# Output products woven between the half products of w_in, in a fused attention and feed-forward kernel

## The chip, the cores and the metric

The kernel runs on one core of a Trainium2 chip. The metric is the device time of one execution in microseconds (us). The engines are called PE (TensorE; its weight loads are shown apart as PEld), DVE (VectorE), ACT (ScalarE), POOL (GpSimd) and SP (SyncE, whose queue issues most transfers).

## The reference

Banded attention (each query sees itself and the 63 keys before it) over 8 batches, 8 heads, 576 positions and 64 columns a head; its result, as 4608 tokens of 512 columns, goes through two matrix products with a leaky ReLU of a slope per column between them:

```python
scores = scale * np.matmul(q, k.transpose(0, 1, 3, 2))
mask = (rel >= 0) & (rel < 64)
attn = softmax(np.where(mask, scores, -1e9))
x = (attn @ v) as (4608, 512)
h = x @ w_in                       # 512 x 2048
g = np.maximum(h, 0.0) + alpha * np.minimum(h, 0.0)
out = (g @ w_out).astype(np.float32)   # 2048 x 512
```

## The kernel before

**Tiles.** The 4608 tokens are 36 tiles of 128; four tiles make a batch (`ts`), nine batches in all (`n`). The 2048 columns between the products are 16 slices of 128 (`f`). Every matrix that goes into a product is held as a high and a low part ("h" and "l", both of type F32R), and a product is made of three: high by high, high by low, low by high.

**The two halves of the program.** Batches 0 and 1 go through `cell`, one slice at a time (L908). Batches 2 to 8 go through `pair`, which makes two slices at once: 7 batches of 8 pairs are 56 pairs. A pair makes the product of x with two slices of w_in out of seven half products instead of eight, from sums and differences of quarters of w_in (kept in DRAM by `combine`, and loaded again for each pair by `load`: the streamed blocks l0 to l4) and of x. A half product (`product`, L1038) is six matmuls of 128x128 weights with 256 columns. In the order of their steps they are: s12 (the first two in one step, so 12 matmuls; it waits for the block l0), s7, s6, s4, s5, s3. The last one needs what v2 adds on DVE from the result of s5. Copies on ACT carry parts of results on: c1 copies the result of s12 and s6 needs it, c7 that of s7 for s4, c6 that of s6 for s5.

**Behind a pair.** For each of its two slices `behind` runs a chain: slopes on ACT (L810), most on DVE (L817), high on ACT (gh, L823), rest on POOL (gl, L827), and the output matmuls (`outs`, L844): per tile gh by wout_h, gh by wout_l, gl by wout_h, 512 columns each, added in the tile's bank over all 16 slices. For pairs these 12 matmuls are three steps of four: gh, gh, gl.

**Attention** of the coming tiles is put in blocks between two pairs: scores (L586), values (L707), scores. It stands behind the last product of one pair and in front of the first of the next.

**The order.** Each step carries, per engine, how long it holds the engine and how long its result takes (`hold, lat`), what it waits for (`after`), what it stands behind in order alone (`behind`), which buffers it takes and gives, and a wish for its time (`want`). `Plan.order` lets a simulated machine, `Plan.run`, pick at each turn the step with the earliest due time (`late`) of those that can start first. The steps are then emitted in the order of the start times so found. Nothing is reordered after that on an engine. A half product holds PE for 0.72 in this plan, an output step for 0.2267 per matmul. Eight PSUM banks are used: four for outputs, four for the half products, scores and values.

Of the kernel before, what the change touches and what calls it, by code (L numbers as in the profile page):

```python
# [3 lines left out]

# [21 lines left out]
WARM = 28.0  # L26
SWITCH = 0.11
SLACK = 1.04


DUE = (
# [77 lines left out]
class Step:  # L109
    def __init__(self, engines, emit, after, behind, take, give, want, moved, span, port):  # L110
        self.engines, self.emit, self.after = engines, emit, [a for a in after if a is not None]
        self.behind, self.take, self.give, self.want, self.moved = behind, take, give, want, moved
        self.span, self.port = span, port
        self.before, self.tiled, self.next = [], False, None
        self.start = self.end = None
        self.late = math.inf


class Plan:
# [47 lines left out]
    def run(self, late):  # L167

        free = {PE: 0.0, DVE: 0.0, ACT: 0.8, POOL: 3.6, SP: 0.8, (DVE, "port"): 3.6, (POOL, "port"): 0.0}
        lanes, flying, tiled = 0.0, [], False  # L170
        left, base, ready, end = {}, {}, [], 0.0

        def open_up(s):
            wants = {}
            for b in s.take:
                wants[b.kind] = wants.get(b.kind, 0) + 1
            base[s] = (max([s.begin] + [a.end + HOP for a in s.after] + [a.start + 0.01 for a in s.behind]), wants)
            ready.append(s)

        for s, x in zip(self.steps, late):  # L180
            s.late, left[s] = x, len(s.after) + len(s.behind)
            if not left[s]:
                open_up(s)
        while ready:
            best = None
            picks = {}
            for s in ready:
                t0, wants = base[s]
                for kind, n in wants.items():
                    have = sorted(self.stock[kind])  # L190
                    t0 = max(t0, have[n - 1][0] + HOP if len(have) >= n else math.inf)
                if s.moved and len(flying) >= FLIGHT:
                    t0 = max(t0, flying[0])
                if t0 == math.inf:
                    continue
                for e in s.engines:
                    t = max(t0, free[e])
                    if e == POOL or s.port and e == DVE:
                        t = max(t, free[e, "port"])
                    picks.setdefault(e, []).append((t, s, e))  # L200
            for e, some in picks.items():
                first = min(x[0] for x in some)
                x = min((x for x in some if x[0] <= first + LOOK), key=lambda x: (x[1].late, x[0]))
                cost = (x[0], x[0] + x[1].engines[e][1], x[1].late)
                if best is None or cost < best[0]:
                    best = cost, x
            if best is None:
                return math.inf
            (_, (t, s, e)) = best
            while s:  # L210
                hold, lat = (x * (1.0 if e == PE else SLACK) for x in s.engines[e])
                while flying and flying[0] <= t:
                    heapq.heappop(flying)
                if e == PE and s.tiled != tiled:
                    tiled, hold, lat = s.tiled, hold + SWITCH, lat + SWITCH
                s.start, s.engine = t, e
                free[e] = t + hold
                if e == POOL or s.port and e == DVE:
                    free[DVE if e == POOL else POOL, "port"] = t + hold
                s.end = t + lat  # L220
                if s.moved:
                    lanes = max(lanes, t + hold + 0.65)
                    s.end = lanes + max(s.moved, s.span) + 0.45
                    lanes += s.moved
                    heapq.heappush(flying, s.end)
                end = max(end, s.end)
                for b in s.take:
                    have = self.stock[b.kind]
                    have.sort()
                    fit = [x for x in have if x[0] + HOP <= t + 1e-9]  # L230
                    x = fit[0]
                    have.remove(x)
                    b.at = x[1]
                for b in s.give:
                    b.uses -= 1
                    b.end = max(b.end, s.end)
                    if not b.uses:
                        self.stock[b.heir or b.kind].append((b.end, b.at))
                ready.remove(s)
                for b in s.before:  # L240
                    left[b] -= 1
                    if not left[b]:
                        open_up(b)
                s, t = s.next, free[e]
        return end

    def filled(self, done):
# [37 lines left out]
def banded_attention_then_prelu_ffn(  # L285
# [11 lines left out]
    nc = tc.nc  # L297
    P = 128
# [7 lines left out]
    NF = DFF // P  # L306
# [496 lines left out]
    def behind(ts, f, d, done, hb, want_o, cols, coarse=True):  # L803
# [28 lines left out]
        if f == NF - 1:  # L832
            todos = [every] if coarse else [every[j:j + 3] for j in range(0, 3 * n, 3)]
        else:
            todos = [gh_ones + gl_ones] if coarse else [gh_ones[:4], gh_ones[4:], gl_ones]

        def outs(todo):
            gh, gl = d["gh"], d.get("gl")
            for i, k in todo:
                t = ts[i]  # L840
                if f == 0 and k == 0:
                    po[t] = bank(ob[t], [P, E], F32, f"o_{t}")
                gt, wt = ((gh, "wout_h"), (gh, "wout_l"), (gl, "wout_h"))[k]
                nc.tensor.matmul(po[t], gt[:, cols[i] * P:(cols[i] + 1) * P], weight(wt, f),  # L844
                                 start=(f == 0 and k == 0), stop=(f == NF - 1 and k == 2))

        hold = {2: (1.46, 0.37, 0.40, 0.31, 0.69), 4: (2.72, 0.57, 0.667, 0.53, 1.24)}[n]
        lat = {2: (1.55, 0.475, 0.485, 0.405, 0.74), 4: (2.87, 0.69, 0.75, 0.62, 1.28)}[n]
# [11 lines left out]
        for todo in todos:  # L860
# [3 lines left out]
            s5 = step({PE: (h, h + 0.1)}, lambda _, todo=todo: outs(todo),  # L864
                      [s3] + [s4] * lows + cv[2 * f + 1]["done"], take=[ob[t] for t in own],
                      give=[ghb] + [glb] * lows, want=want_o)
            for x in {id(last_o[t]): last_o[t] for t in ts if t in last_o}.values():
                put_behind(s5, x)
            for t in ts:
# [129 lines left out]
    def pair(ts, q, want):  # L999
# [34 lines left out]
        def product(out, w, x, start):  # L1034
            todo = [(w[i], x[j]) for i, j in ((0, 0), (0, 1), (1, 0))]
            for i, (a, b) in enumerate(todo):
                for c in range(2):
                    nc.tensor.matmul(out, a[:, c * P:(c + 1) * P], b[c], start=start and i == c == 0,  # L1038
                                     stop=i == 2 and c == 1, skip_group_check=True)

        def p12(_):
            dx["h"] = bank(bx, [P, NBLK * P], F32, f"h_{ts[0]}_{f}")
            d["b"], d["a"] = dx["h"][:, :2 * P], dx["h"][:, 2 * P:]
            product(d["a"], own(0, 0), tokens(0, left), True)
            product(d["b"], streamed(0), tokens(1, left), False)

        def p7(_):
            dy["h"] = bank(by, [P, NBLK * P], F32, f"h_{ts[0]}_{f + 1}")
            d["d"], d["c"] = dy["h"][:, :2 * P], dy["h"][:, 2 * P:]
            product(d["d"], streamed(3), tokens(0, right), True)  # L1050

        def p6(_):
            product(d["a"], streamed(1), turned(2), False)

        def p5(_):
            product(d["a"], streamed(4), turned(0), False)

        def p3(_):
            product(d["a"], streamed(2), tokens(1, right), False)

        def p4(_):
            product(d["d"], own(1, 1), turned(1), False)

        def add(out, a, b):
            nc.vector.tensor_tensor(out=out, in0=a, in1=b, op=ALU.add)  # L1065
# [11 lines left out]
        (l0, b0), (l3, b3), (l1, b1), (l4, b4), (l2, b2) = (load(e) for e in (0, 3, 1, 4, 2))  # L1077
        x0, x1, x2, x3 = (st[t]["x"] for t in ts)
        one = {PE: (0.72, 0.91)}
        s12 = step({PE: (1.44, 1.63)}, p12, [st_done[t] for t in ts] + [l0], take=[bx], give=[b0, x0, x2], want=want)  # L1080
        s7 = step(one, p7, [l3], [s12], take=[by], give=[b3, x1, x3], want=want + 1.0)
        c1 = step({ACT: (0.28, 0.39)}, lambda _: spare(0, "a"), [s12], take=[u2])
        c7 = step({ACT: (0.28, 0.39)}, lambda _: spare(2, "d"), [s7], [c1], take=[u7])
        s6 = step(one, p6, [c1, l1], [s7], give=[b1, tsets[n]], want=want + 2.0)
        c6 = step({ACT: (0.28, 0.39)}, lambda _: spare(1, "a"), [s6, c1])
        s4 = step(one, p4, [c7], [s6], give=[tsets[n]], want=want + 3.0)
        s5 = step(one, p5, [c6, l4], [s4], give=[b4, tsets[n]], want=want + 4.0)
        v2 = step({DVE: (0.38, 0.48)}, lambda _: add(d["c"], d["a"], d["u7"]), [s5, c7, s4], give=[u7])
        s3 = step(one, p3, [v2, l2], give=[b2, x1, x3], want=want + 5.0)
        v3 = step({DVE: (0.38, 0.48)}, lambda _: add(d["d"], d["d"], d["u"][1]), [s4, c6, v2], give=[u2])  # L1090
        v1 = step({DVE: (0.38, 0.48)}, lambda _: add(d["b"], d["b"], d["u"][0]), [c1, s3], give=[u2])
        first[n, f] = first[n, f + 1] = s12
        last_p[n, f] = s3
        if q == 0:
            for b, m in zip((x0, x1, x2, x3), (1, 2, 1, 2)):
                b.uses = m * NF // 2
# [2 lines left out]
        behind(ts, f, dx, [s3, v1], bx, want + LAGS[0], cols, False)  # L1099
        behind(ts, f + 1, dy, [v2, v3], by, want + LAGS[1], cols, False)  # L1100

    tsets, loaded, last_p = {}, [], {}
    regions, taken, begun = {}, {}, []
    borrowed = [Buffer(f"x{i}", 4 * LENT) for i in range(NBLK)]
    for i, q0 in enumerate(TSETS):
# [58 lines left out]
    for n in range(NB):  # L1164
# [12 lines left out]
        for f in range(NF):  # L1177
# [11 lines left out]
            if (n, f) in stays:  # L1189
# [14 lines left out]
                    end = x  # L1204
                stay = f, end

    with tc.manual_schedule():
        for s in plan.order():
            s.emit(s.engine)


# [39 lines left out]
```

## Time and profile before

| what | value |
|---|---|
| three runs | 875.98, 877.21, 878.53 us, median 877.21 |
| the profiled execution | 877.72 us, of which a span of 876.0 us from the first to the last instruction |
| granted clock of TensorE | 1.000 of 2.4 GHz |
| busy share of the span | PE 99%, PEld 87%, DVE 64%, ACT 53%, POOL 41% |

A busy share tells how long an engine had at least one instruction under way. Matmuls overlap in the array, so that the spacing of their starts, not their durations, tells how fast they go.

### The profile page before, as it was taken

How to read it: one execution, taken by the hardware profiler on the slowest of the kernel's cores; microseconds unless marked ns; L12 is line 12 of the kernel's file. 1: busy time of each engine (PE TensorE's matmuls, PEld its weight loads, DVE VectorE, ACT ScalarE, POOL GpSimd, SP SyncE). 2: the span in 40 equal slices, each digit the busy share in tenths (PEclk: the TensorE clock that was granted, in tenths of full speed). 3: DMA queues.
4: the chain of work that ended last, by engine and by line, in shares of the span. 5: the costliest groups of instructions: out<-in, count | busy, mean ns of one | idle time of the engine just before them, and what ended most of it. 6: DMA issues, size and time to landing. Idle time of an engine off the chain costs nothing.

```text
span 876.0 us, 20755 instructions
## 1 busy us (share of the span) xinstructions
PE 867.1 (99%) x7793; PEld 764.2 (87%) x7793; DVE 557.2 (64%) x1611; ACT 465.4 (53%) x1245; POOL 359.0 (41%) x328
## 2 busy tenths in 40 slices
PE   8999999999999999999999999999999999999998
PEld 7888878888889898999898989989898989999997
DVE  5889978978675666657583848384856666423221
ACT  6888767456363636364544536363636363434333
POOL 4878665885433332333241333233323323222222
PEclk9999999999999999999999999999999999999999
DMA  9666857555765566645664576446655564345441
GB/s 312 196 191 198 255 148 240 152 176 172 246 202 167 149 190 195 191 136 164 211 190 131 151 237 202 141 131 216 196 166 148 190 196 130 110 126 175 121 121 61
DMA packets 106739, 153.93 MB, mean 176 GB/s; under 512 B 8704, under 2 KB 64272, under 8 KB 106640
## 3 DMA queue, kind: packets, MB, share of 16 engines
q1 hardware_dynamic: 105904, 151.95, 56.2%
q8 instruction: 62, 1.02, 0.5%
q10 hardware_dynamic: 736, 0.66, 0.2%
q14 instruction: 37, 0.30, 0.1%
HBM read 132.65 MB, written 19.92 MB: 174 GB/s over the span
## 4 chain that ended last, share of the span: by engine, by line
PE 97%; DVE 1%; DMA 1%; ACT 1%; issue 0%; POOL 0%; ACTq 0%; DVEq 0%; POOLq 0%
PE o L844 45%; PE h L1038 32%; PE h L908 10%; PE av L707 4%; PE s L586 3%; PE s L568 1%; DMA q<-qT 1%; PE t L664 1%; PE spare L377 0%; ACT w L616 0%; DVE w L610 0%; DVE two L412 0%; ACT pt L669 0%; POOL w L647 0%; ACTq L510 0%
## 5 line engine op out<-in xcount | busy, mean ns | idle before, releaser
L827 POOL TENSOR_TENSOR gl<-g,gh 128x512 fp32r<-128x512 f32 x128 | 165.5, 1294 | 409.4 <-ACT gh L823 244.3
L844 PE MATMUL o<-wout_h,gh 128*128 128x512 f32 x576 | 228.2, 396 | 0.0
L844 PE MATMUL o<-wout_l,gh 128*128 128x512 f32 x576 | 225.6, 392 | 0.0
L810 ACT ACTIVATE g<-h,sa_sb 128x512 f32<-128x512 f32 (+1 forms) x148 | 100.2, 677 | 160.9 <-DVE h L1065 139.0
L844 PE MATMUL o<-wout_h,gl 128*128 128x512 f32 x576 | 159.5, 390 | 0.0
L687 DVE STREAM_TRANSPOSE pt<-w 32x256 f32<-32x256 f32 x312 | 129.4, 427 | 6.0 <-POOL w L647 0.8
L844 PEld LDWEIGHTS o<-wout_h,gl 128*128 128x128 f32 x576 | 107.9, 188 | 23.2
L844 PEld LDWEIGHTS o<-wout_h,gh 128*128 128x128 f32 x576 | 108.5, 188 | 20.9 <-issue 0.5
L817 DVE SCALAR_TENSOR_TENSOR g<-h,s_sb,g 128x512 f32<-128x512 f32 x128 | 95.8, 749 | 45.2 <-ACT g L810 42.3
L844 PEld LDWEIGHTS o<-wout_l,gh 128*128 128x128 f32 x576 | 108.5, 188 | 18.4
L823 ACT CAST gh<-g 128x512 fp32r<-128x512 f32 x128 | 79.5, 621 | 79.4 <-DVE g L817 79.4
L1065 DVE TENSOR_TENSOR h<-h,w 128x256 f32<-128x256 f32 x56 | 24.2, 432 | 142.8 <-PE h L1038 142.4
L626 ACT ACTIVATE w<-w,nm 128x96 f32<-128x96 f32 x208 | 75.6, 366 | 15.5 <-DVE nm L620 15.5
L647 POOL TENSOR_TENSOR w<-w,rc 128x768 f32<-128x768 f32 (+2 forms) x44 | 59.3, 1348 | 56.5 <-DVE rc L643 53.8
L1075 ACT COPY u<-h 128x256 f32<-128x256 f32 x112 | 41.8, 373 | 76.2 <-PE h L1038 76.1
L1065 DVE TENSOR_TENSOR h<-h,u 128x256 f32<-128x256 f32 x112 | 48.0, 428 | 31.0 <-PE h L1038 25.6
L1038 PE MATMUL h<-xh,win_l 128*128 128x256 f32 x336 | 67.5, 283 | 0.0
L1038 PE MATMUL h<-xh,win_h 128*128 128x256 f32 x336 | 67.5, 282 | 0.0
L1038 PE MATMUL h<-win_h,win_l 128*128 128x256 f32 x336 | 58.8, 283 | 0.0
L1038 PEld LDWEIGHTS h<-xh,win_h 128*128 128x128 f32 x336 | 55.1, 191 | 3.4
L1038 PEld LDWEIGHTS h<-xh,win_l 128*128 128x128 f32 x336 | 53.1, 192 | 0.9
L1038 PE MATMUL h<-win_h,win_h 128*128 128x256 f32 x252 | 51.5, 295 | 0.1
(122 smaller groups left out, 1528.5 us busy)
## 6 DMA issues: line engine op xcount, KB each, us to landing
win_h<-kept SPq DMA_DIRECT2D x112, 256.0 KB, 3.0
win_l<-kept SPq DMA_DIRECT2D x112, 256.0 KB, 2.9
v<-vN SPq DMA_DIRECT2D x72, 256.0 KB, 4.6
stream<-kept SPq DMA_DIRECT2D x56, 256.0 KB, 2.7
k<-kT SPq DMA_DIRECT2D x35, 384.0 KB, 4.2
out<-os SPq DMA_DIRECT2D x35, 256.0 KB, 3.2
q<-qT SPq DMA_DIRECT2D x34, 256.0 KB, 4.3
raw<-w_in SPq DMA_DIRECT2D x16, 512.0 KB, 4.7
```

Source lines behind the costliest of these rows:

```text
L626: nc.scalar.activation(w, w, AF.Exp, scale=-1.0, bias=d["nm"][:, g:g + 1], accum_out=d["sm"][:, g:g + 1])
L647: nc.gpsimd.tensor_tensor(out=w, in0=w, in1=d["rc"][:, g].unsqueeze(2).broadcast_to(list(w.shape)), op=ALU.mult)
L687: nc.vector.transpose(dst[:, :, i * SUB:(i + 1) * SUB], d["w"][r, :, :, k * SUB:(k + 1) * SUB].rearrange("p e h k -> p (e h) k"))
L810: nc.scalar.activation(d["g"], d["h"][:, :nt], AF.Copy, scale=sa_sb[:, f:f + 1])
L817: nc.vector.scalar_tensor_tensor(out=g, in0=d["h"][:, :nt], scalar=s_sb[:, f:f + 1], in1=d["g"], op0=ALU.mult, op1=ALU.max)
L823: nc.scalar.copy(d["gh"], d["g"])
L827: (nc.vector if start else nc.gpsimd).tensor_tensor(out=d["gl"], in0=d["g"], in1=d["gh"].bitcast(F32), op=ALU.subtract)
L844: nc.tensor.matmul(po[t], gt[:, cols[i] * P:(cols[i] + 1) * P], weight(wt, f), start=(f == 0 and k == 0), stop=(f == NF - 1 and k == 2))
L908: nc.tensor.matmul(ph[:, :nt], weight(wt, f)[:, c * P:(c + 1) * P], tokens_of(xt, xs)[:, c], start=(k == 0), stop=(k == 3 * NP - 1))
L1038: nc.tensor.matmul(out, a[:, c * P:(c + 1) * P], b[c], start=start and i == c == 0, stop=i == 2 and c == 1, skip_group_check=True)
L1065: nc.vector.tensor_tensor(out=out, in0=a, in1=b, op=ALU.add)
L1075: nc.scalar.copy(d["u"][i], d[x])
```

## The change

Output steps of pairs become groups of three matmuls (`todos`). Half products (kind "h", now seven steps a pair, s12 split into s1 and s12) and output groups (kind "o") can be mated by the planner: when it picks one of them and one of the other kind could start at that time, both are emitted as one, an output matmul in front of every two of the half product. A half product takes a mate only when more than `keep` output groups have their inputs ready; `KEEP` gives that number for each of the seven. The plan counts a mated couple as `GAIN` = 0.024 shorter than its parts. The first half product doesn't wait for the streamed block any more, and stands behind the sixth product of the pair before (`before[-1:]`). The times of the three copies in the plan are lengthened.

```diff
+GAIN = 0.024
+KEEP = (1, 1, 1, 1, 1, 2, 2)
...
+        outs = [s for s in self.steps if s.kind == 'o']
...
+            if s.kind:
+                mates = [x for x, t0 in times.items() if x.kind and x.kind != s.kind and t0 <= t]
+                s.mate = min(mates, key=lambda x: x.late, default=None)
+                if s.mate:
+                    x = s if s.kind == "h" else s.mate
+                    fit = [o for o in outs if o.start is None and all(a.end is not None and a.end <= t for a in o.after)]
+                    if len(fit) <= x.keep:
+                        s.mate = None
+                if s.mate:
+                    s.next, s.mate.next, s.mate.mate = s.mate, s.next, s
...
+                if s.mate and not twin:
+                    twin = s.mate
+                    both = hold + s.mate.engines[e][0] - GAIN
+                    hold, lat = both, lat - hold + both
+                elif s is twin:
+                    hold, lat, twin = both, lat - hold + both, None
...
-            todos = [gh_ones + gl_ones] if coarse else [gh_ones[:4], gh_ones[4:], gl_ones]
+            todos = [gh_ones + gl_ones] if coarse else [(gh_ones + gl_ones)[j:j + 3] for j in range(0, 3 * n, 3)]
...
+            if not coarse:
+                s5.kind = "o"
...
-        s12 = step({PE: (1.44, 1.63)}, p12, [st_done[t] for t in ts] + [l0], take=[bx], give=[b0, x0, x2], want=want)
+        s1 = step(one, p1, [st_done[t] for t in ts], before[-1:], take=[bx], give=[x0], want=want)
+        s12 = step(one, p2, [l0], [s1], give=[b0, x2], want=want + 0.5)
...
-        c1 = step({ACT: (0.28, 0.39)}, lambda _: spare(0, "a"), [s12], take=[u2])
-        c7 = step({ACT: (0.28, 0.39)}, lambda _: spare(2, "d"), [s7], [c1], take=[u7])
+        c1 = step({ACT: (0.28, 0.46)}, lambda _: spare(0, "a"), [s12], take=[u2])
+        c7 = step({ACT: (0.28, 0.44)}, lambda _: spare(2, "d"), [s7], [c1], take=[u7])
...
-        c6 = step({ACT: (0.28, 0.39)}, lambda _: spare(1, "a"), [s6, c1])
+        c6 = step({ACT: (0.28, 0.44)}, lambda _: spare(1, "a"), [s6, c1])
...
-        first[n, f] = first[n, f + 1] = s12
+        first[n, f] = first[n, f + 1] = s1
+        for x, m in zip((s1, s12, s7, s6, s4, s5, s3), KEEP):
+            x.kind, x.keep = "h", m
...
+        before.append(s5)
...
+    def weave(some, others):
+        for _ in others:
+            for _ in range(2):
+                next(some)
+        for _ in some:
+            pass
...
         for s in plan.order():
-            s.emit(s.engine)
+            if s.mate and s.kind == "o":
+                continue
+            some = s.emit(s.engine)
+            if s.kind or inspect.isgenerator(some):
+                weave(some, s.mate.emit(PE) if s.mate else ())
```

`product` and `outs` yield after each matmul, so that `weave` can take an output matmul, then two of the half product, and so on.

## Rows read from the trace of the kernel before

**Rows 1.** The page: busy time per engine, and the chain that ended last.
```profile
PE 867.1 (99%) x7793; PEld 764.2 (87%) x7793; DVE 557.2 (64%) x1611; ACT 465.4 (53%) x1245; POOL 359.0 (41%) x328
...
PE 97%; DVE 1%; DMA 1%; ACT 1%; issue 0%; POOL 0%; ACTq 0%; DVEq 0%; POOLq 0%
PE o L844 45%; PE h L1038 32%; PE h L908 10%; PE av L707 4%; PE s L586 3%; PE s L568 1%; DMA q<-qT 1%; PE t L664 1%; PE spare L377 0%; ACT w L616 0%; DVE w L610 0%; DVE two L412 0%; ACT pt L669 0%; POOL w L647 0%; ACTq L510 0%
```
**Rows 2.** Windows: length, busy of PE, PEld, DVE, ACT, POOL, clock, DMA.
```profile
248.00:862.00 614.00, 613.20 (x5628) 552.50 (x5625) 356.36 (x1030) 293.11 (x791) 188.39 (x169) 1.00 0.55 165
```
**Rows 3.** Waits of PE from 225 us on: total, times, longest.
```profile
PE s L586 <- issue: 0.7, 3, 0.3
PE h L1038 <- DVE h L1065: 0.6, 1, 0.6
```
**Rows 4.** Chain in order of time, 480 to 530: start, length, what.
```profile
483.72 4.41 PE h L1038 x36
...
494.34 4.37 PE h L1038 x36
498.71 2.74 PE o L844 x12
501.44 0.71 PE h L1038 x6
502.16 2.75 PE o L844 x12
...
516.91 2.87 PE h L1038 x24
519.78 0.93 PE o L844 x4
...
521.42 2.73 PE o L844 x12
```
**Rows 5.** Timeline of PE, 493.9 to 505: start, length, matmuls that follow each other.
```profile
494.65 0.40 PE L1038 MATMUL h<-xh,win_l 128*128 128x256 f32 x2
...
496.09 0.40 PE L1038 MATMUL h<-xh,win_l 128*128 128x256 f32 x2
496.32 0.47 PE L1038 MATMUL h<-win_h,win_h 128*128 128x256 f32 x2
496.63 0.40 PE L1038 MATMUL h<-win_l,win_h 128*128 128x256 f32 x2
...
499.24 0.39 PE L844 MATMUL o<-wout_l,gh 128*128 128x512 f32 x1
...
501.28 0.40 PE L1038 MATMUL h<-xh,stream 128*128 128x256 f32 x2
501.51 0.40 PE L1038 MATMUL h<-xl,stream 128*128 128x256 f32 x2
501.75 0.40 PE L1038 MATMUL h<-xh,stream 128*128 128x256 f32 x2
```
**Rows 6.** Timeline of PE: the first matmuls of a run of four outputs.
```profile
519.62 0.39 PE L844 MATMUL o<-wout_h,gh 128*128 128x512 f32 x1
519.85 0.39 PE L844 MATMUL o<-wout_l,gh 128*128 128x512 f32 x1
```
**Rows 7.** Timeline of weight loads: the first two of s6, in the pair from 494.18.
```profile
496.29 0.30 PEld L1038 LDWEIGHTS h<-win_h,win_h 128*128 128x128 f32 x2
```
**Rows 8.** Timeline of ACT: the copy c1 of that pair.
```profile
495.86 0.37 ACT L1075 COPY u<-h 128x256 f32<-128x256 f32 x1 [1.45 <-PE h L1038]
```
**Rows 9.** Timeline of DVE: v2 of that pair.
```profile
498.81 0.43 DVE L1065 TENSOR_TENSOR h<-h,w 128x256 f32<-128x256 f32 x1 [0.92 <-PE h L1038]
```
**Rows 10.** Chain in order of time: the last run of matmuls.
```profile
862.27 10.07 PE o L844 x44
```
**Rows 11.** Timeline of ACT: the last cast to gh.
```profile
864.40 0.62 ACT L823 CAST gh<-g 128x512 fp32r<-128x512 f32 x1 [0.35 <-DVE g L817]
```
**Rows 12.** Timeline of weight loads: the first output behind a run of h.
```profile
501.88 0.19 PEld L844 LDWEIGHTS o<-wout_h,gh 128*128 128x128 f32 x1
```

More of the change, by code (lines that the diff above doesn't have):

```diff
@@ L1 @@
 import heapq
+import inspect
 import math
@@ L113, in __init__ @@
         self.span, self.port = span, port
-        self.before, self.tiled, self.next = [], False, None
+        self.before, self.tiled, self.next, self.kind, self.mate, self.keep = [], False, None, None, None, 0
         self.start = self.end = None
@@ L183, in run @@
                 open_up(s)
+        outs = [s for s in self.steps if s.kind == 'o']
         while ready:
             best = None
-            picks = {}
+            picks, times = {}, {}
             for s in ready:
@@ L195, in run @@
                     continue
+                times[s] = t0
                 for e in s.engines:
@@ L209, in run @@
             (_, (t, s, e)) = best
+            if s.kind:
[8 more added lines that the diff above has]
+                    s.next, s.mate.next, s.mate.mate = s.mate, s.next, s
+            twin = None
             while s:
@@ L243, in run @@
                         open_up(b)
-                s, t = s.next, free[e]
+                s, t = s.next, t if twin else free[e]
         return end
@@ L843, in outs @@
                 gt, wt = ((gh, "wout_h"), (gh, "wout_l"), (gl, "wout_h"))[k]
-                nc.tensor.matmul(po[t], gt[:, cols[i] * P:(cols[i] + 1) * P], weight(wt, f),
-                                 start=(f == 0 and k == 0), stop=(f == NF - 1 and k == 2))
+                yield nc.tensor.matmul(po[t], gt[:, cols[i] * P:(cols[i] + 1) * P], weight(wt, f),
+                                       start=(f == 0 and k == 0), stop=(f == NF - 1 and k == 2))
         hold = {2: (1.46, 0.37, 0.40, 0.31, 0.69), 4: (2.72, 0.57, 0.667, 0.53, 1.24)}[n]
@@ L1037, in product, with p1, p2 @@
                 for c in range(2):
-                    nc.tensor.matmul(out, a[:, c * P:(c + 1) * P], b[c], start=start and i == c == 0,
-                                     stop=i == 2 and c == 1, skip_group_check=True)
-        def p12(_):
+                    yield nc.tensor.matmul(out, a[:, c * P:(c + 1) * P], b[c], start=start and i == c == 0,
+                                           stop=i == 2 and c == 1, skip_group_check=True)
+        def p1(_):
             dx["h"] = bank(bx, [P, NBLK * P], F32, f"h_{ts[0]}_{f}")
             d["b"], d["a"] = dx["h"][:, :2 * P], dx["h"][:, 2 * P:]
-            product(d["a"], own(0, 0), tokens(0, left), True)
-            product(d["b"], streamed(0), tokens(1, left), False)
+            yield from product(d["a"], own(0, 0), tokens(0, left), True)
+        def p2(_):
+            yield from product(d["b"], streamed(0), tokens(1, left), False)
         def p7(_):
@@ L1049, in p7 @@
             d["d"], d["c"] = dy["h"][:, :2 * P], dy["h"][:, 2 * P:]
-            product(d["d"], streamed(3), tokens(0, right), True)
+            yield from product(d["d"], streamed(3), tokens(0, right), True)
         def p6(_):
-            product(d["a"], streamed(1), turned(2), False)
+            yield from product(d["a"], streamed(1), turned(2), False)
         def p5(_):
-            product(d["a"], streamed(4), turned(0), False)
+            yield from product(d["a"], streamed(4), turned(0), False)
         def p3(_):
-            product(d["a"], streamed(2), tokens(1, right), False)
+            yield from product(d["a"], streamed(2), tokens(1, right), False)
         def p4(_):
-            product(d["d"], own(1, 1), turned(1), False)
+            yield from product(d["d"], own(1, 1), turned(1), False)
         def add(out, a, b):
@@ L1100, in pair @@
         behind(ts, f + 1, dy, [v2, v3], by, want + LAGS[1], cols, False)
-    tsets, loaded, last_p = {}, [], {}
+    tsets, loaded, last_p, before = {}, [], {}, []
     regions, taken, begun = {}, {}, []
```

## The prediction

> **What bounds the kernel now.** I read the page first: TensorE is busy 99% of the span, and the chain that ended last lies on it for 97%, most of that in the output matmuls of L844 and the half-product matmuls of L1038 [rows 1]. The stage in which the change works runs from about 232 us to the end; for its main part the windows view gives TensorE 613.20 of 614.00 us busy, at a granted clock of 1.00 (2.4 GHz) throughout [rows 2]. The view of waits leaves TensorE with little more than 1 us of idle time there [rows 3]. So nothing is to be had from another engine; the time is a sum of matmul spacings, and the only question is whether the same matmuls in another order stand closer together. A busy share can't answer that, because a matmul that starts late behind its weight load, or waits inside the array, still counts as busy. So I went on to the chain in order of time, which gives the runs of equal matmuls and their lengths [rows 4], and to the starts in the timeline [rows 5, 6].
>
> A usual pair of 42 half matmuls (h) and 24 output matmuls (o) takes 4.37 us for 36 h, 2.74 for 12 o, 0.71 for the last six h, 2.75 for 12 o: 10.57 us [rows 4]. In the middle of a run, twelve h take 496.09 - 494.65 = 1.44 us, 0.120 each; nine o (499.24 to 501.28) take 2.04, 0.2267 each [rows 5]. At these spacings a pair would take 42 x 0.120 + 24 x 0.2267 = 10.48. The 0.09 above that is of two kinds:
>
> - A stall in the run of 36 h. The load that opens the fourth product, s6, stands at 496.29 [rows 7], where the last matmul of the product before starts at 496.21 (the row of two from 496.09) and a load elsewhere follows that start at once. It waits for the copy c1, which ends at 495.86 + 0.37 = 496.23 [rows 8]. Two h then take 496.63 - 496.32 = 0.31 instead of 0.24 [rows 5]. That is 0.07 a pair, in 43 of the 56 pairs; 11 of these have 4.41 instead of 4.37. The other 13 have the run cut, as 18 and 24 h, and the 24 take 2.87, less than 24 x 0.120 = 2.88 [rows 4].
> - The borders. The first two h behind an o take 0.23 (501.28 to 501.51), the next two 0.24 [rows 5], and six take 0.71 instead of 0.72 [rows 4]: an h run gives back about 0.008. Against this the 12 o behind it take 2.74 or 2.75 instead of 2.72, and four take 0.93 instead of 0.907 [rows 4]. An o run pays 0.015 to 0.03, some 0.003 to 0.007 for each of its first matmuls.
>
> **The change part by part.** No matmul, copy or transfer is added or left out. The matmuls of a pair stand as o, h, h, o, h, h in place of long runs.
>
> *How much is woven.* A pair has seven half products and eight output groups of three. A product is woven only when more groups are ready than its KEEP asks for. Behind the sixth product, v2 must run before the seventh: the run of h ends at 494.34 + 4.37 = 498.71 [rows 4], v2 at 499.24 [rows 9], and the load of the next product comes behind that. One group of 3 x 0.2267 = 0.68 us hardly covers the 0.53; KEEP leaves two. That leaves six groups for weaving, which I take: 18 trios of o, h, h, one product alone, two groups alone. Over 56 pairs that is 1008 trios; the first pair has no such groups in front of it, which I let pass.
>
> *What a trio costs.* The trace before has no single o between h, so I bound it. In long runs a trio is 0.2267 + 0.240 = 0.467. Lower end: both h stand first behind an o and give back 0.008, and the o, with only two h before it, pays nothing: 0.459. Upper end: the o pays the most that one matmul of a short run shows beyond that, and the h give nothing back: 0.475. The nearest row is the shortest o run, four o between h: its first takes 519.85 - 519.62 = 0.23 [rows 6], so 0.003 are paid; the h give back 0.008 as all 45 runs of six do. I take 0.462.
>
> *Sum.* A woven pair: 18 x 0.462 = 8.32, one product alone 0.71, two groups alone 1.36 + 0.02 = 1.38; together 10.41. The stall isn't in it: c1 has a woven s7 of 1.38 us behind it instead of 0.72, and the later copies likewise; where a product goes unwoven for want of groups, the 0.07 comes back. Against 10.57 that is 0.16; in the 13 cut pairs 0.09; 11 pairs had 0.04 more to lose. 43 x 0.16 + 13 x 0.09 + 11 x 0.04 = 8.5 us.
>
> *What is given back at the end.* Now 44 o stand behind the last h for 10.07 us [rows 10], and the last gh is made from 864.40 to 865.02 [rows 11], 2.8 us into that run, so that it is covered. With the older groups woven away, two groups (1.36) and those of the other cell stand there; that cell's cast ends 1 us before the last one's. I count 0.6 us of idle time. Some pairs will find fewer groups; 0.4 for that. Net gain 7.5 us.
>
> *Parts at no cost.* Splitting the first two products apart frees the first from its wait for the streamed block, and puts it behind the sixth product of the pair before. No wait for that block shows above the waits named [rows 3], so I count nothing; its price, were transfers late, is a wait in the second product instead. The regrouped outputs ask for gl one group sooner; POOL is busy 41% [rows 1], and first groups of other cells cover it. Both h banks of a pair are held longer; that is the rival below.
>
> The profiled execution took 877.72 us with a span of 876.0; the median of the three runs is 877.21. Gains are differences, so I take them from the median: 877.2 - 7.5 = 869.7, said as **869.5**. The three runs spread over 0.3%, so 0.3% (2.6 us) is about what a measurement tells from no change.
>
> **Rivals.**
>
> *The trio gives its full 0.459.* Then 1008 x 0.003 = 3.0 us more: 866.5. For it: an o at the end of a run shows no payment. Against: every first o behind h shows some.
>
> *The weave returns nothing.* A weight load starts as the matmul before it starts: the load for the o behind two h stands at 501.88, the second of the two h from 501.75 at 501.87 [rows 5, 12]. So only one load is ever ahead, and what an h can hide is the load behind it. In six h and three o, six loads stand behind an h and three behind an o, woven or not. If the load sets the 0.120, a trio stays at 0.467: 5.0 us less gained, 874.5, from the stalls alone. Against: the 0.23 above.
> The Trainium skill, TensorE: Matmul & The Clock Gate, section LDWEIGHTS, puts a load at its columns over 1.2 GHz, an estimate of 107 ns for 128, as long as 256 columns take at 2.4 GHz. By that rule the weave has nothing to hide better and the time is 874.5; the trace agrees in so far as h stand at 0.120 and not lower.
>
> *Slower: the attention blocks lose their cover.* Twelve blocks stand between two pairs, behind the last product of one and in front of the first of the next. In front of one stand 12 o, 2.73 us [rows 4], while DVE and ACT bring the finished pair out of its two banks, which the scores and values need. Woven, perhaps two groups (1.36) stand there. If nothing else is ready, 2.73 - 1.36 = 1.4 us are idle in each: 12 x 1.4 = 16 us, 886. It decides from 7.5 / 12 = 0.6 us a block. Against: a pair's first cell is finished before its last product and brings groups of its own. A trio at 0.475 would end there too: 1008 x 0.013 = 13 us, 882.5.
>
> **How the numbers follow.** Chances: 0.44 for the forecast, 0.24 for the full 0.459, 0.18 for no return, 0.14 for slower. The forecast's case reaches from 867 to 872. The range takes in 866.5 with 4 us below it (more groups woven, or a trio of 0.455), and 874.5 with 3 above: 862.5 to 877.5. No return falls about evenly on both sides of 0.3%: faster 0.44 + 0.24 + 0.07 = 0.75, same 0.11, slower 0.14.
>
> **What would show it.** In the timeline of the changed kernel: starts of o to o, over two h, of 0.46 (right), 0.467 (no return), over 0.47 (wrong sign); the load at the fourth product no longer late; a pair near 10.4 us; waits of TensorE below 3 us in all, at the end above all. If idle time stands around L586 and L707, the blocks are the cause; if pairs show half of their products alone, too few groups were ready and my 1008 is wrong.

## The result and the profile after

The changed kernel takes 881.69 us (four runs, 881.40 to 882.02) against 876.60 for the kernel before measured beside it; the ratio is 1.0051, with a 95% interval from 1.0037 to 1.0065. It is 0.5% slower, clear of that interval, where 869.5 was forecast, and it lies outside the range.

The profiled execution took 881.4 us, with a span of 879.7. The page (busy time, and the waits that the page puts in front of a group of L866, the old L844; L1062 is the old L1038, L904 the copy of a finished output tile to `os`):

```profile
PE 867.7 (99%) x7793; PEld 759.5 (86%) x7793; DVE 557.9 (63%) x1605; ACT 463.3 (53%) x1251; POOL 359.9 (41%) x328
...
PE 84%; DMA 5%; DVE 2%; ACT 2%; issue 1%; POOL 0%; ACTq 0%; DVEq 0%; POOLq 0%
...
L866 PE MATMUL o<-wout_h,gh 128*128 128x512 f32 x576 | 228.8, 397 | 4.0 <-ACT os L904 3.9
```

TensorE has the same busy share as in [rows 1], but the chain that ended last now leaves it: 5% go to a DMA, which was 1% (by the page's next line 3% of the span is stores, out<-os, and the rest transfers near the start), and an output matmul waits for ACT. The 3% aren't the loss: TensorE works on beside most of a store. In the view of waits of the whole changed kernel (total, times, longest) and, under it, of the kernel before:

```profile
ACT os L904 <- DMA out<-os: 16.1, 8, 2.3
PEld o L866 <- ACT os L904: 5.2, 6, 1.0
PE o L866 <- ACT os L904: 3.9, 5, 0.8
```

```profile
DVE os L882 <- DMA out<-os: 4.8, 3, 1.7
...
ACT os L880 <- DMA out<-os: 0.2, 1, 0.2
```

One of these places in the changed kernel, first in the chain in order of time, then in the timelines of SP, ACT and TensorE:

```profile
329.87 4.41 DMA out<-os
...
334.38 0.59 ACT os L904
...
335.02 3.02 PE o L866 x12
```

```profile
328.47 0.34 SPq L909 DMA_DIRECT2D out<-os  x1
...
329.87 3.01 SPq L909 DMA_DIRECT2D out<-os  x2
```

```profile
331.93 0.59 ACT L904 COPY os<-o 128x512 f32<-128x512 f32 x1 [2.17 <-PE o L866]
334.38 0.59 ACT L904 COPY os<-o 128x512 f32<-128x512 f32 x1 [1.86 <-DMA out<-os]
```

```profile
331.52 0.40 PE L866 MATMUL o<-wout_h,gl 128*128 128x512 f32 x1
331.75 0.40 PE L1062 MATMUL h<-win_h,win_l 128*128 128x256 f32 x2
331.99 0.39 PE L866 MATMUL o<-wout_h,gh 128*128 128x512 f32 x1
...
333.38 0.39 PE L1062 MATMUL h<-xh,win_h 128*128 128x256 f32 x2
333.61 0.40 PE L1062 MATMUL h<-xl,win_h 128*128 128x256 f32 x2
333.84 0.40 PE L1062 MATMUL h<-xh,win_h 128*128 128x256 f32 x2
335.02 0.50 PE L866 MATMUL o<-wout_h,gh 128*128 128x512 f32 x1 [0.78 <-ACT os L904]
```

This is the change from one batch to the next. The four output tiles of the old batch are copied to `os`, which has two buffers, and stored. The store issued at 329.87 lands 4.41 us later; only then can the fourth copy begin (334.38), which frees the fourth output bank. The old batch's last output matmul starts at 331.52, and the new batch's first one, at 331.99, stands only two h behind it. The first two output groups of the new batch (six o) find the three banks that are free; then comes a half product that isn't woven (six h); and the third group, which opens a run of 12 o, needs the fourth bank and stands on TensorE with everything behind it. Without the wait it would have started 0.12 behind the last h, at 334.08: 0.94 us are lost. There are five such places, some 94 us apart, and a smaller one; the weight loads are idle for 5.2 us there.

The same place in the kernel before, in the timelines of DVE and TensorE:

```profile
331.50 1.34 DVE L882 COPY os<-o 128x512 f32<-128x512 f32 x2 [1.61 <-DMA out<-os]
```

```profile
330.13 0.39 PE L844 MATMUL o<-wout_h,gl 128*128 128x512 f32 x1
...
333.23 0.39 PE L844 MATMUL o<-wout_h,gh 128*128 128x512 f32 x1
...
335.33 0.40 PE L844 MATMUL o<-wout_h,gh 128*128 128x512 f32 x1
```

A copy waits for a store here too. But 24 h stand between the old batch's last output matmul (330.13) and the new batch's first (333.23), and the last copy ends at 332.84, 2.5 us before the fourth bank is asked for (335.33).

The woven part itself, in the timeline of TensorE and of the weight loads in the changed kernel:

```profile
326.85 0.40 PE L866 MATMUL o<-wout_l,gh 128*128 128x512 f32 x1
...
328.25 0.39 PE L866 MATMUL o<-wout_l,gh 128*128 128x512 f32 x1
328.48 0.40 PE L1062 MATMUL h<-win_l,win_h 128*128 128x256 f32 x2
328.72 0.40 PE L866 MATMUL o<-wout_h,gl 128*128 128x512 f32 x1
...
331.52 0.40 PE L866 MATMUL o<-wout_h,gl 128*128 128x512 f32 x1
```

```profile
328.26 0.42 PEld L1062 LDWEIGHTS h<-win_l,win_h 128*128 128x128 f32 x2
328.60 0.19 PEld L866 LDWEIGHTS o<-wout_h,gl 128*128 128x128 f32 x1
328.72 0.42 PEld L1062 LDWEIGHTS h<-win_h,win_h 128*128 128x128 f32 x2
```

Ten trios, from 326.85 to 331.52, take 4.67 us, 0.467 each; the mean over the 800 trios between others is 0.468. That is the long runs' 0.2267 + 0.240 [rows 5], not 0.462. The o takes 0.23, the two h 0.24. As before ([rows 12]) each load stands at the start of the matmul in front of it.

Pair by pair: the first half product of the first pair starts at 226.21 (before 227.35), and from there to the end of the span it is 653.5 us against 648.7, 4.8 more. The waits for a bank give some 5.0 of that.

### The profile page after: what moved, and what is told of

It is laid out like the page before. It is cut to its first block, busy times and chain, and to the rows that moved or that the text cites. A ratio compares the mean times of both kernels' runs of the same rounds, so it can differ in the third digit from the quotient of the medians.

```text
span 879.7 us, 20764 instructions
## 1 busy us (share of the span) xinstructions
PE 867.7 (99%) x7793; PEld 759.5 (86%) x7793; DVE 557.9 (63%) x1605; ACT 463.3 (53%) x1251; POOL 359.9 (41%) x328
## 4 chain that ended last, share of the span: by engine, by line
PE 84%; DMA 5%; DVE 2%; ACT 2%; issue 1%; POOL 0%; ACTq 0%; DVEq 0%; POOLq 0%
PE o L866 41%; PE h L1062 29%; PE h L932 7%; PE av L729 4%; DMA out<-os 3%; PE s L608 3%; DMA raw<-w_in 1%; DMA raw<-w_out 1%; ACT os L904 1%; PE s L590 0%; DVE os L906 0%; DVE g L839 0%; DVE h L1091 0%; ACT two L432 0%; ACT u L1101 0%
## 5 line engine op out<-in xcount | busy, mean ns | idle before, releaser
L866 PE MATMUL o<-wout_h,gh 128*128 128x512 f32 x576 | 228.8, 397 | 4.0 <-ACT os L904 3.9
L866 PE MATMUL o<-wout_l,gh 128*128 128x512 f32 x576 | 226.6, 393 | 0.0
L866 PE MATMUL o<-wout_h,gl 128*128 128x512 f32 x576 | 194.7, 393 | 0.0
L866 PEld LDWEIGHTS o<-wout_h,gh 128*128 128x128 f32 x576 | 108.2, 188 | 17.2 <-ACT os L904 5.2
L866 PEld LDWEIGHTS o<-wout_h,gl 128*128 128x128 f32 x576 | 107.0, 188 | 11.8
L866 PEld LDWEIGHTS o<-wout_l,gh 128*128 128x128 f32 x576 | 108.6, 188 | 9.5
L1062 PE MATMUL h<-xh,win_h 128*128 128x256 f32 x340 | 67.6, 280 | 0.0
L1062 PEld LDWEIGHTS h<-xh,win_h 128*128 128x128 f32 x340 | 61.1, 188 | 6.7
L1062 PE MATMUL h<-xh,win_l 128*128 128x256 f32 x336 | 66.9, 281 | 0.0
L1062 PEld LDWEIGHTS h<-xh,win_l 128*128 128x128 f32 x336 | 60.7, 188 | 5.8
L1062 PE MATMUL h<-win_h,win_l 128*128 128x256 f32 x336 | 65.0, 281 | 0.0
L1062 PEld LDWEIGHTS h<-win_h,win_l 128*128 128x128 f32 x336 | 59.6, 188 | 5.9
```

Of the source, the lines that this page charges most:

```text
L866: yield nc.tensor.matmul(po[t], gt[:, cols[i] * P:(cols[i] + 1) * P], weight(wt, f), start=(f == 0 and k == 0), stop=(f == NF - 1 and k == 2))
L1062: yield nc.tensor.matmul(out, a[:, c * P:(c + 1) * P], b[c], start=start and i == c == 0, stop=i == 2 and c == 1, skip_group_check=True)
```

## The experiments

All times are medians beside runs of the kernel before on the same chip, where that took 876.9 to 877.4.

**The same plan, unwoven, outputs first (o_first).**

```diff
         for _ in others:
-            for _ in range(2):
-                next(some)
+            pass
         for _ in some:
             pass
```

> The changed kernel with the same plan, but a mated couple is emitted as its three output matmuls and then its six half-product matmuls, not woven. Theory A (the weave returns nothing; the changed kernel lost through five waits of about 0.93 us for an output bank at the change of a batch): the trio is 0.468 in the changed kernel, 0.467 in runs, 846 trios x 0.001 = 1 us, so 880 to 882.5, and the five waits stay, since an output is still the first of its couple. Rival B (the output matmul between half products is what costs): 878 or less. Rival C (the weave does return its 0.008 a trio, and all of the loss lies elsewhere): 846 x 0.008 = 6.8 us slower, 888.

Measured: 882.45 us, ratio 1.0051 (1.0034 to 1.0068). The waits are there as well:

```profile
PE o L866 <- ACT os L904: 4.0, 6, 0.8
```

So the loss doesn't hang on the weave, and weaving neither costs nor returns several us; rivals B and C fall. Against the spacings of long runs, all intervals of o and h that are less than 0.05 too long add up to 3.0 us too much in this kernel and 1.8 in the woven one: a run of three o and six h pays at its border somewhat more than three trios do.

**The same plan, unwoven, half product first (h_first).**

```diff
-        for _ in others:
-            for _ in range(2):
-                next(some)
         for _ in some:
             pass
+        for _ in others:
+            pass
```

> The same, but a couple is emitted as its six half-product matmuls and then its three output matmuls. Theory A: in front of the output that waits for its bank now stand 0.70 us of half-product matmuls, so five waits of 0.93 shrink to about 0.2: 881.7 - 3.6 - 1 = 877 to 878. If the bank isn't what is waited for but the place in the plan is, the waits stay and it is 880 to 882.

Measured: 877.07 us, ratio 0.9995 (0.9982 to 1.0008), the number of theory A, but not for its reason. The view of TensorE's waits begins with

```profile
PE spare L399 <- DVE xl L398: 1.1, 1, 1.1
PE s L608 <- issue: 1.0, 3, 0.5
```

and has no output among them. ACT's copies still wait for stores at the same place in the plan (timelines of SP, ACT and TensorE):

```profile
330.82 1.94 SPq L909 DMA_DIRECT2D out<-os  x2
```

```profile
333.49 0.59 ACT L904 COPY os<-o 128x512 f32<-128x512 f32 x1 [1.09 <-DMA out<-os]
```

```profile
334.09 0.40 PE L1062 MATMUL h<-xh,win_h 128*128 128x256 f32 x2
...
334.80 0.40 PE L866 MATMUL o<-wout_h,gh 128*128 128x512 f32 x1
```

Theory A put 0.7 us of half product in front of the output that waits. But that output wasn't mated: six h stood in front of it in the woven kernel too (from 333.38), and what stands there is the same. What is new is the store: issued at 330.82, it lands after 2.6 us instead of 4.41, so that the copy ends at 334.08, before the output's turn at 334.80. At the five changes that waited, the first two stores of the old batch land after 2.3 to 2.7 us here and 3.1 to 4.4 in the woven kernel. So early outputs alone cost nothing; they cost where the stores land late as well. That theory A's number came out is luck.

**Woven, with a third place for a finished tile (os_in_gh).**

```diff
-                    sbuf, os = Buffer("g" if t == NT - 1 else "gh" if t == NT - 2 else "os", 1), {}
+                    sbuf, os = Buffer("g" if t == NT - 1 else "gh" if t == NT - 2 else "gh" if t >= W0 * NBLK and i == 3 else "os", 1), {}
```

> The changed kernel, woven, but the last of the four output tiles of a batch (batches 2 to 8) is copied to a free gh buffer instead of one of the two os buffers, so that its copy need not wait for a store to land. Theory A: the five waits of 0.93 go and the trio stays at 0.468: 881.7 - 4.7 = 877, no faster than the kernel before (876.6). Rival D (the waits only move to another buffer or bank, since the outputs are now made as early as they can be): 880 to 882.

Measured: 875.47 us, ratio 0.9981 (0.9970 to 0.9993). TensorE's waits for ACT's copies are gone from the view, and 6 us with them, though the second store of a batch lands as late as before (4.25 to 4.50 us at the same five changes). So the loss comes about where early outputs meet a buffer that waits for its store. As rival D has it, a wait moves, to ACT's casts,

```profile
ACT gh L845 <- DMA out<-os: 5.0, 5, 1.4
```

but TensorE's view shows no wait from it. The kernel is now 1.7 us faster than the kernel before, which theory A didn't forecast. The waits were some 5.0 of the 6 us; another 1.1 is in the stalls from h to h, which add up to 2.7 us in this trace and 3.8 in that of the woven kernel, as this plan comes out somewhat otherwise.

**No mates (no_mates).** Everything of the change but the weave and the early outputs.

```diff
-            if s.kind:
+            if s.kind and False:
```

> The changed kernel without mates: groups of three, first product on its own and free of its streamed block, longer copies in the plan, but no output matmul woven. Theory A: neither the gain nor the waits at the change of a batch come from these parts; the outputs keep their late places: 875 to 878, as the kernel before. Rival E (the regrouping, or the first product's new place, brings the waits): 880 or more, with the same waits for an output bank.

Measured: 876.70 us, ratio 0.9990 (0.9980 to 1.0000). Groups of three and the first product's new place don't bring the waits: without mates ACT's copies wait for stores for 0.2 us in all, as before. In its timeline 24 h stand between the old batch's last output matmul and the new batch's first, as in the kernel before. It is the mating, which takes an output group that is ready and doesn't wait until it is due, that puts the new batch's outputs right behind the old batch's.

**Half products on 128 columns (half_width).** On the kernel before; five of six matmuls of a half product leave out half of their columns.

```diff
-                    nc.tensor.matmul(out, a[:, c * P:(c + 1) * P], b[c], ...
+                    w = 2 * P if i == c == 0 else P
+                    nc.tensor.matmul(out[:, :w], a[:, c * P:(c + 1) * P], b[c][:, :w], ...
```

> The kernel before with five of the six matmuls of each half product of a pair on 128 columns instead of 256 (half of their product is left out, so the output is another one); their weight loads stay as they are. It tells what sets the 0.120 from h to h. If the load of the next weights sets it: 0.117 to 0.120 as before, and the kernel takes 870 to 877. If the columns and a fixed cost for each matmul set it (0.013 and 256 columns at 2.4 GHz in 0.107, as 0.2267 for 512 has it): 0.067, and 56 x 35 x 0.053 = 104 us less, 773, unless another engine then sets the time.

Measured: 861.29 us in one run. In its timelines, TensorE and then loads:

```profile
494.39 0.39 PE L1039 MATMUL h<-xl,stream 128*128 128x128 f32 x2
494.61 0.39 PE L1039 MATMUL h<-xh,stream 128*128 128x128 f32 x2
494.83 0.45 PE L844 MATMUL o<-wout_h,gh 128*128 128x512 f32 x1
```

```profile
494.33 0.30 PEld L1039 LDWEIGHTS h<-xl,stream 128*128 128x128 f32 x2
494.55 0.30 PEld L1039 LDWEIGHTS h<-xh,stream 128*128 128x128 f32 x2
494.78 0.19 PEld L844 LDWEIGHTS o<-wout_h,gh 128*128 128x128 f32 x1
```

Two h of half the columns take 0.22 instead of 0.24, and two loads stand 0.22 apart: about 0.11 each (median 0.112). So there is a floor of 0.112 under every h, and 256 columns lie only 0.008 above it. By that 56 x 35 x 0.008 = 15.7 us, and 876.9 - 861.3 = 15.6, but the agreement is in part chance: in the two traces the spacings behind an h add up to 22 us less and those from o to o to 6 more. The first answer of the expectation was nearer, but not whole: the 0.120 itself still fits the columns and a fixed 0.013. What sets the floor, this run doesn't isolate. The load of 128 columns of weights, which it left as it was, is the likely one. A fixed price for each matmul doesn't fit, since the attention's matmuls L707, with 64 columns of weights and 64 to multiply, stand 0.032 apart (64 in 2.02 us in the chain of late_c1). The Trainium skill, TensorE: Matmul & The Clock Gate, section LDWEIGHTS, puts a load at its columns over 1.2 GHz, an estimate of 107 ns for 128; the 0.11 from load to load agrees.

**The longer copies in the plan alone (late_copies).** On the kernel before.

```diff
-        c1 = step({ACT: (0.28, 0.39)}, ...
+        c1 = step({ACT: (0.28, 0.46)}, ...
```

The times of c7 and c6 are set to 0.44 in the same way.

> The kernel before with only the longer times of the three copies in the plan (c1 0.46, c7 and c6 0.44), one part of the change alone. Theory A: this part is neither the loss nor a gain of the changed kernel, since the plan only counts a wait that it takes anyway: 875 to 878. If the longer times lead the plan to put outputs in front of s6, the stall of 0.07 goes in 43 pairs: 873 to 874.

Measured: 876.87 us, ratio 1.0000 (0.9991 to 1.0010). No loss, no gain from this part.

**The return of the weave by itself (gh_h_first).** os_in_gh with couples emitted as in h_first.

> The kernel with the last output tile of a batch copied to a gh buffer (875.5, no waits for an output bank), with mated couples emitted as six half-product matmuls and then three outputs, not woven. It gives the return of the weave by itself, without the waits. Theory A: none or nearly none, by the runs so far 280 couples x 0.004 = 1.1 us in favour of the weave: 875.5 to 877.5. If the weave returns 0.024 a couple: 280 x 0.024 = 6.7 us, 882.

Measured: 875.43 us, ratio 0.9982 (0.9973 to 0.9992); woven it was 875.47, ratio 0.9981. With the waits away the weave returns nothing that can be measured; by the two intervals, the 6.7 us are ruled out and the 1.1 are not.

**Fewer couples (gh_keep9).** os_in_gh with

```diff
-KEEP = (1, 1, 1, 1, 1, 2, 2)
+KEEP = (1, 1, 1, 1, 1, 9, 9)
```

> The kernel with the last output tile of a batch copied to a gh buffer, woven, with KEEP 9 for the sixth and the seventh product, so that these go unwoven and some 212 couples are left instead of 284. Theory A: the weave returns nothing, so a quarter of it fewer costs nothing: 874.5 to 876.5. If each couple returns 0.024: 72 x 0.024 = 1.7 us slower, 877.

Measured: 875.82 us, ratio 0.9994 (0.9984 to 1.0004). Inconclusive by itself: the time fits no return, but the ratio is 0.0013 (1.1 us) above that of os_in_gh, with intervals that overlap, and so it doesn't rule out the smaller return either.

**The stall at s6 by itself (late_c1).** On the kernel before.

```diff
-        c1 = step({ACT: (0.28, 0.39)}, ...
+        c1 = step({ACT: (0.28, 0.53)}, ...
```

> The kernel before, with only the time of the copy c1 in the plan set from 0.39 to 0.53, so that the plan finds s6 too late and puts outputs in front of it. It tests the other term of the prediction, the stall of 0.07 us in 43 pairs, by itself. If the stall is worth what the rows said: 43 x 0.07 + 11 x 0.04 = 3.4 us less, 873.5. If it only moves to a later product of the pair: 876 to 877.

Measured: 874.48 us, ratio 0.9976 (0.9963 to 0.9988), by one number in the plan. It is the lowest median of the kernels that compute the whole result, though its interval overlaps those of os_in_gh, gh_h_first and gh_c1_56. Its chain in order of time around a pair:

```profile
491.88 2.15 PE h L1038 x18
494.03 0.93 PE o L844 x4
494.96 2.15 PE h L1038 x18
497.11 1.84 PE o L844 x8
498.95 0.71 PE h L1038 x6
499.67 2.75 PE o L844 x12
```

Four o stand in front of s6, and 36 h take 2.15 + 2.15 = 4.30 instead of 4.37 [rows 4]. A border more costs 0.02 of it (0.93 for four o), and the pair takes 10.53 instead of 10.57.

**The rest of that stall in the woven kernel (gh_c1_56).** os_in_gh with c1 at 0.56 in the plan instead of 0.46.

> The woven kernel with the last output tile of a batch copied to a gh buffer (875.5), with c1 at 0.56 in the plan instead of 0.46. By its trace some stalls at s6 are left, of 0.15 us in most batches and 0.4 in two pairs: 875.5 - 1 to 1.5 = 874 to 874.5 if the plan puts outputs in front of those too; 875.5 if not.

Measured: 875.04 us, ratio 0.9979 (0.9969 to 0.9989). No difference from os_in_gh that can be told. The stalls are still there: intervals from h to h that are over 0.025 too long add up to 2.7 us in both traces. Why the plan doesn't put outputs there isn't shown.

## Why the prediction was wrong

**What bounds the kernel** was read rightly: a sum of spacings on TensorE. But the answer was not only in the spacings. Three steps failed: the trio was priced too low, the stall at s6 was counted as gone, and the output banks were in no term of the sum.

**The trio, 0.462, was mis-sized: 0.468 measured.** The step took two prices from borders of long runs and added them. Of these the payment of the o is there (0.232 from o to h instead of 0.2267), the return of the h isn't: the first h to the second takes 0.117 in a trio, not 0.113 as behind a run of o, and the second to the next o 0.119. Sum 0.468. In the kernel before the h gave back 0.007 to 0.008 behind runs of four o or more; behind a single o that itself stands behind h, 0.004 are left, and the o takes 0.005. half_width bounds what an h can give back: even with half of its columns it stands at 0.112, 0.008 lower. The rival "the weave returns nothing" was right on this term, and gh_h_first against os_in_gh shows it. By that rival's own price it takes 5.0 us from the forecast gain.

**1008 trios** were 867 (289 of 392 half products woven, counted in the trace; the expectation's 846 is too low); with nothing measurable returned by each this moved no time.

**The stall at s6, 3.4 us, was priced rightly and freed only in part.** In late_c1 the intervals from h to h that are over 0.025 too long fall from 4.9 us to 1.2; the smaller excesses, which stand at the borders of runs above all, grow by 1.3, and the kernel gets 2.1 us (by the ratio) to 2.6 us (by the medians) faster. In the changed kernel they still add up to 3.8: the stall stays in pairs whose s7 goes unwoven. "Where a product goes unwoven for want of groups, the 0.07 comes back" was said, and priced at 0.4 us with the rest; it came back larger, 0.37 in some pairs, since ACT has the other cells' work in front of c1 there (timelines of the changed kernel, ACT and TensorE):

```profile
356.27 0.62 ACT L845 CAST gh<-g 128x512 fp32r<-128x512 f32 x1
356.80 0.37 ACT L1101 COPY u<-h 128x256 f32<-128x256 f32 x1
```

```profile
356.71 0.40 PE L1062 MATMUL h<-xh,win_l 128*128 128x256 f32 x2
357.22 0.50 PE L1062 MATMUL h<-win_h,win_h 128*128 128x256 f32 x2
```

**The largest loss was in no term.** I looked for the time that earlier outputs cost among what the half products and the scores need (h banks, attention's cover, the tail), and found three places for it. None is there: scores wait 0.7 us for issue, and the last run of o is closed to its end (54 in 12.34 us). The rival of the attention blocks gave 882.5 to 886, close to what was measured, but its mechanism isn't the one at work. The place was among what the outputs need themselves, which "Parts at no cost" leaves out without a reason: the four output banks, which pass from one batch to the next through a copy, two `os` buffers and a store. That is worth 5.0 us. The profile before could have told it: DVE's copies waited 4.8 us for stores, and TensorE felt nothing of it because the fourth bank was free some 2.5 us before it was asked for. That margin comes from 24 h between the two batches' outputs, and the wish of `LAGS` puts a pair's outputs 16 to 19 us behind its products. The mating rule picks among the groups that can start without waiting for that wish. The plan counts 2.3 us from issue to landing for a store that finds the queue free (0.42 + 0.65 + 0.8 + 0.45 in `Plan.run`); the one that held up the bank took 4.41.

**The terms together.** Of the forecast gain of 7.5 us, 5.0 go with the weave, 2.3 with the stall (3.4 forecast, 1.1 freed) and 5.0 with the waits for a bank; 0.6 come back because the end shows no idle time. That makes 4.2 us slower, against 4.8 from the first pair to the end. Without the waits (os_in_gh) the kernel takes 875.5, near the 874.5 that "no return" gave.

What stays open: why a trio's h give back half of what they do behind a run of o; the spacings are shown, their cause isn't. And why the first two stores of a batch land after 3.1 to 4.4 us at five changes in the woven kernel, after 2.0 to 2.5 in the kernel before and 2.3 to 2.7 in h_first. In the example above two loads and two stores of 256 KB are issued from 327.98 to 329.87, within 1.9 us, against 2.8 us in h_first (328.00 to 330.82), but no run isolates this.

## What to carry to other kernels

When a change takes work earlier than it is due, ask what that work takes and who gives it back: list its output buffers too, back to the transfer that frees them, with the landing time from the trace and not from the plan. Before blaming the order alone, look when the transfer lands: here the same early outputs cost 5 us with late stores and nothing with early ones. Don't add the prices of borders of long runs to get that of a fine interleaving: here 0.462 was added up and 0.468 measured. And a stall with a cheap cause (one copy 0.07 us late, in 43 places) is best tried alone before the large change that covers it in passing.

## What the hardware showed that was not expected

With new weights for each matmul, 256 columns take 0.120 and 128 take 0.112 on average: halving the columns of a short matmul gives back a fifteenth. A store of 256 KB landed 4.41 us after its issue, where the median of all such stores in that kernel is 3.4, and where the same tile's store took 2.1 us in the kernel before.
